# V on unnormalized probabilities, scaled later by reciprocals that pass through DRAM, in a top-k attention and SwiGLU kernel

## The chip, the core and the metric

The kernel runs on one core of a Trainium2 chip. TensorE (PE, with its weight loads as PEld), VectorE (DVE), ScalarE (ACT) and GpSimd (POOL) each work through their own instructions in order; SyncE (SP) issues nearly all DMAs. The metric is the device time of one execution in microseconds, given as the median of several runs.

## The reference

Inputs are q, k and v of 8 batches x 8 heads x 576 positions x 64, and three FFN weights. All is float32.

```python
scores = (q @ k.transpose(0, 1, 3, 2)) / np.sqrt(64)
kth = np.partition(scores, -32, axis=-1)[..., -32:-31]
scores = np.where(scores >= kth, scores, -1e9)          # the 32 largest of each row
scores = scores - scores.max(axis=-1, keepdims=True)
attn = np.exp(scores)
attn = attn / (attn.sum(axis=-1, keepdims=True) + 1e-9)
x = (attn @ v)            # (B,H,S,D) -> (B*S, H*D) = (4608, 512)
g = x @ w_gate            # 512 -> 1536
out = (g * sigmoid(g) * (x @ w_val)) @ w_out            # -> (4608, 512)
```

## The kernel before

**Units.** Attention is cut into 160 units: 8 batches x 5 query tiles x 4 pairs of heads. Query tiles 0 to 3 have 128 rows, and their units carry both heads of the pair, 1152 scores a row. Tile 4 has the last 64 rows; its two heads share the 128 partitions, so that unit is a "one-head" unit with 576 scores a row and half the work. In each batch 16 two-head units are followed by 4 one-head units.

**Steps of a unit.** `scores` (PE L308 or L294, copied to `sc` by ACT L313 or L299); `select` (DVE: four rounds of MAX8 L329 with three MATCH_REPLACE8 L333 between, for each head, then L339, which writes a large negative penalty into `e` where a score is below the 32nd); `penalize` (POOL L349, L351: adds the scores to the penalty); `weigh` (ACT exp L360 with the row sums in `tot`, and L365, which adds 1e-9); `normalize` (DVE reciprocal L372, ACT multiply L375, in place); `turn` (PE transposes L387 of the nine 128-column blocks of `e` into three PSUM tiles `etps`: four blocks, one, four; ACT copies L388 to `et`); `values` (PE L407 for the last 64 positions of both heads, L416 for the rest; ACT copy L431 into `xT`, the FFN's input).

**FFN.** `feed` works on blocks of 256 tokens. A block can begin when `values` has filled its `xT` for all four head pairs. Its matmuls are L471 (w_gate and w_val, 96 products of 128x128 by 256 columns, each two passes) and, behind block 0, seven quarters through L557 (42 products). ACT L496 to L503 and POOL L499, L504 and sums take the results. It is a generator: `pieces(n)` emits up to n pieces (four L471 products, or about that) while a credit lasts. `share(n)` gives the credit of a turn, about 6.4 pieces less the cost of PE's other work in it; a turn's unused credit is carried to a small extent, and nothing is emitted while no block is complete.

**Order.** The order on PE, DVE, ACT and POOL is that of the program: the last lines of the kernel chain each engine's instructions. SP's DMAs are placed by a scheduler. Turn n of the main loop (L729) emits `select` of unit n in parts, and beside it: at the head `penalize(n-1)`, `turn(n-3)`, `values(n-4)`, the scores of n+1, `weigh(n-1)`; then pieces, the reciprocal and multiplies of `normalize(n-2)`, key and query transposes for n+2 (`prep`, L255 to L268) where a new head pair begins, and more pieces. In the instruction order a two-head turn's tail and the next head read on PE: FFN, nine L387, L407 and eight L416 of the unit before, L308, FFN. The weights are rounded in the first turns (`rounded`, L105 to L123), by ACT, DVE and POOL.

**Buffers.** `sc` has 2, `e` 4, `et` 2, `tot` 3; PSUM has five tiles for attention (`ps_t`) and three for the FFN (`ps_f`).

Of the kernel before, what the change touches and what calls it, by code (L numbers as in the profile page):

```python
# [8 lines left out]
AF = mybir.ActivationFunctionType  # L9
# [6 lines left out]
P = 128  # L16
# [9 lines left out]
def kernel(  # L26
# [58 lines left out]
    ffn = ctx.enter_context(tc.tile_pool(name="ffn", bufs=2))  # L85
    ps_t = ctx.enter_context(tc.tile_pool(name="ps_t", bufs=5, space=PSUM))
    ps_f = ctx.enter_context(tc.tile_pool(name="ps_f", bufs=3, space=PSUM))

    ident = consts.tile([P, P], FP32, name="ident")
    make_identity(nc, ident[:])  # L90
# [2 lines left out]
    for i in range(NV):  # L93
        vt = consts.tile([P, P], FP32, name=f"vlast{i}")
        nc.vector.memset(vt[:], 0.0)
        vlast.append(vt)
    eps = consts.tile([P, 1], FP32, name="eps")
    nc.vector.memset(eps[:], EPS)
    wg = consts.tile([P, KC, DFF], FP32, name="wg")
    wv = consts.tile([P, KC, DFF], FP32, name="wv")  # L100
    wo = consts.tile([P, MC, DM], FP32, name="wo")
# [176 lines left out]
    def scores(n):  # L278
        b, qt, hp = units[n]
        slab = preps[b * NHP + hp]  # L280
        sc = work.tile([P, 2 * S], FP32, tag="sc", name="sc", bufs=2)
        halves = [slice(0, D), slice(D, P)]
        half = S // 2

        def bank():
            return ps_t.tile([P, 512], FP32, tag="t", name="s")


        if qt == J:
            banks = [bank() for _ in range(2)]  # L290
            for i, ps in enumerate(banks):
                for d in halves:
                    k0 = R + i * half
                    nc.tensor.matmul(  # L294
                        ps[d, 0:half], slab[d, S + R : S + 2 * R], slab[d, k0 : k0 + half]
                    )
            yield
            for i, ps in enumerate(banks):
                nc.scalar.copy(sc[:, i * half : (i + 1) * half], ps[:, 0:half])  # L299
        else:  # L300
            q0 = S + 2 * R + qt * P
            banks = []
            for i in range(2):
                for hh, d in enumerate(halves):
                    ps = bank()
                    banks.append((i + 2 * hh, ps))
                    k0 = (1 - hh) * R + i * half
                    nc.tensor.matmul(  # L308
                        ps[:, 0:half], slab[d, q0 : q0 + P], slab[d, k0 : k0 + half]
                    )  # L310
            yield
            for i, ps in banks:
                nc.scalar.copy(sc[:, i * half : (i + 1) * half], ps[:, 0:half])  # L313
        state[n] = dict(sc=sc)

    def select(n):

        nh = n_heads(units[n][1])
        sc = state[n]["sc"]
        m = small.tile([P, 2, TOP_K], FP32, tag="m", name="m", bufs=2)  # L320
        heads = [slice(t * S, (t + 1) * S) for t in range(nh)]
        rest = work.tile([P, 2 * S], FP32, tag="rest", name="rest", bufs=1)
        e = work.tile([P, 2 * S], FP32, tag="e", name="e", bufs=4)
        state[n] |= dict(m=m, e=e, heads=heads)
        cur = sc
        rounds = TOP_K // 8
        for r in range(rounds):
            for t, hs in enumerate(heads):
                nc.vector.max(m[:, t, 8 * r : 8 * r + 8], cur[:, hs])  # L329
                yield  # L330
            if r < rounds - 1:
                for t, hs in enumerate(heads):
                    nc.vector.match_replace(  # L333
                        rest[:, hs], m[:, t, 8 * r : 8 * r + 8], cur[:, hs], LOWEST
                    )
                    yield
                cur = rest
        for t, hs in enumerate(heads):
            nc.vector.tensor_scalar(  # L339
                e[:, hs], sc[:, hs], m[:, t, TOP_K - 1 : TOP_K], FAR, ALU.is_lt, ALU.mult  # L340
            )
# [12 lines left out]
    def weigh(n):  # L354

        st = state[n]
        e, heads, bias = st["e"], st["heads"], st.pop("bias")
        tot = small.tile([P, 2], FP32, tag="tot", name="tot")
        for t, hs in enumerate(heads):
            nc.scalar.activation(  # L360
                e[:, hs], e[:, hs], AF.Exp, bias=bias[:, t : t + 1], scale=scale,
                accum_out=tot[:, t : t + 1],
            )
        nh = len(heads)
        nc.scalar.activation(tot[:, 0:nh], tot[:, 0:nh], AF.Identity, bias=eps[:])  # L365
        st["tot"] = tot

    def normalize(n):
        st = state[n]
        tot, e, heads = st.pop("tot"), st["e"], st.pop("heads")  # L370
        nh = len(heads)
        nc.vector.reciprocal(tot[:, 0:nh], tot[:, 0:nh])  # L372
        yield
        for t, hs in enumerate(heads):
            nc.scalar.mul(e[:, hs], e[:, hs], tot[:, t : t + 1])  # L375

    def turn(n):

# [19 lines left out]
    def values(n):  # L398

        b, qt, hp = units[n]  # L400
        vt, v_last, vl = vs[b * NHP + hp]
        et = state.pop(n)["et"]
        last = qt == J
        ql = R if last else P
        av = ps_t.tile([P, P], FP32, tag="t", name="av")
        if not last:
            nc.tensor.matmul(av[:], vl[:], et[:, J, :], start=True, stop=False)  # L407
        for c in range(J + 1 if last else J):
            kl = R if c == J else P
            for hh in range(2):  # L410
                moving = (
                    et[0:kl, c, hh * R : (hh + 1) * R]
                    if last
                    else et[:, c + hh * (J + 1), :]
                )
                nc.tensor.matmul(  # L416
                    av[hh * R : (hh + 1) * R, 0:ql],
                    v_last[:, hh, :] if c == J else vt[:, hh, c, :],
                    moving,
                    start=last and c == 0,  # L420
                    stop=c == (J if last else J - 1),
                )
        c0 = b * S + qt * P
        at = c0
        while at < c0 + ql:
            kb = at // BLK
            n_c = min((kb + 1) * BLK, c0 + ql) - at
            if kb not in xT:
                xT[kb] = ffn.tile([P, NHP, BLK], FP32, tag="xT", name="xT", bufs=3)
                done[kb] = 0  # L430
            nc.scalar.copy(  # L431
                xT[kb][:, hp, at - kb * BLK : at - kb * BLK + n_c],
                av[:, at - c0 : at - c0 + n_c],
            )
            done[kb] += n_c
            at += n_c
# [265 lines left out]
    def pieces(n):  # L702
        for _ in range(n):
            if credit[0] >= 1:
                credit[0] -= piece()

    def run(steps):
        for _ in steps:
            pass

    def finish_unit(n):
        values(n)
        b, qt, hp = units[n]
        if qt == J and b + 1 < B:
            load_v((b + 1) * NHP + hp)
# [7 lines left out]
    run(fetch(1))  # L723
    credit = [0.0]
    no = iter(())
    over = {}
    TURN, VALUES = 3, 4
    due = [2.0]
    for n in range(NU + VALUES):  # L729
        nh = n_heads(units[n][1]) if n < NU else 1  # L730
        topk = select(n) if n < NU else no
        over[n - 1] = normalize(n - 1) if 0 <= n - 1 < NU else no
        nxt = scores(n + 1) if n + 1 < NU else no
        ahead = fetch(n + 2) if n + 2 < NU else no
        norm = over.pop(n - 2, no)

        def dve(k, beside=True):

            for _ in range(k * nh):
                next(topk, None)  # L740
                due[0] += 5 / 6 if beside else 0
                if due[0] >= 1:
                    due[0] -= 1
                    rounding(1)

        if n >= NU - NHP:
            credit[0] = 8.0
        else:
            credit[0] = min(credit[0] + share(n), share(n) + 1)
        flush(on_act)  # L750
        if 0 <= n - 1 < NU:
            penalize(n - 1)
        flush(on_pool)
        if 0 <= n - TURN < NU:
            run(turn(n - TURN))
        if n >= VALUES:
            finish_unit(n - VALUES)
        next(nxt, None)

        early[0]()  # L760
        if 0 <= n - 1 < NU:
            weigh(n - 1)
        run(nxt)


        dve(2, beside=False)
        if 2 <= n + 2 < NHP:
            load(n + 2)
        if n < NHP:
            load_v(n)  # L770
        pieces(2)
        flush(on_act)
        dve(1)
        dve(1)
        next(norm, None)
        run(norm)

        flush(on_pool)
        next(ahead, None)
        pieces(1)  # L780
        next(ahead, None)
        dve(1)
        pieces(1)
        dve(2, beside=False)
        run(topk)
        pieces(6)
    while piece():
        pass
# [48 lines left out]
```

## Time and profile before

| | |
|---|---|
| median of 3 runs | 1820.12 us (1819.79 to 1821.86) |
| profiled execution, first to last instruction | 1817.8 us |
| PE busy | 1708.7 us (94%) |
| DVE busy | 1610.7 us (89%) |
| ACT busy | 1218.7 us (67%) |
| POOL busy | 1036.4 us (57%) |
| mean granted TensorE clock | 0.967 |
| DMA | 59.65 MB, mean 33 GB/s |

The profiled execution shows its own span, 1817.8 us; what lies around it (start and end of the launch) is not in the page, and the median of the runs is 2.3 us above it. The page cuts the span into 40 slices of 45 us, each digit being the busy share in tenths. A timeline row reads: start in us, duration in us, engine, line, operation, output tile <- input tiles, sizes, xcount of merged instructions, and in brackets the engine's idle time just before with what ended it. Merged matmul rows overlap, since matmuls are pipelined: the pace is read from one row's start to the next row's start.

### The profile page before, as it was taken

Reading aid. Unit: us, or ns where it says so; the run is one execution under the profiler, and the core shown is the slowest. Engines: PE = TensorE matmul, PEld = TensorE weight load, DVE = VectorE, ACT = ScalarE, POOL = GpSimd, SP = SyncE. Lnnn points to the kernel's source line nnn. Section 1 sums busy time; section 2 is a strip of 40 time slices with the busy share of each in tenths; the row PEclk is TensorE's granted clock in tenths of the full one; section 3 lists DMA queues with packets and bytes.
Section 4 is the critical chain, followed back from the end, with each engine's and each line's share of the span. In section 5 each row is a group of like instructions: output and inputs, shape, how many; then the busy total and the mean of one; then the engine's idle time right before and its main releaser. Section 6 shows DMA issues by size and latency. Waiting matters only on the chain.

```text
span 1817.8 us, 30526 instructions
## 1 busy us (share of the span) xinstructions
PE 1708.7 (94%) x10756; PEld 1409.2 (78%) x10756; DVE 1610.7 (89%) x3372; ACT 1218.7 (67%) x2977; POOL 1036.4 (57%) x930
## 2 busy tenths in 40 slices
PE   4458999899999899999999999999999999999999
PEld 2346778687788788887888878887888878888887
DVE  7999999999999799997999989998999989998400
ACT  6778666676667676666767676767676766675532
POOL 5788756455565645554455636564556554646354
PEclk6669999899999999999999999999999999999999
DMA  7432030002100030000300021000300011000000
GB/s 191 125 108 90 14 85 7 12 1 50 45 1 13 2 82 12 13 1 22 73 12 2 13 56 39 1 12 3 74 19 13 1 36 33 1 13 12 1 12 12
DMA packets 109305, 59.65 MB, mean 33 GB/s; under 512 B 88544, under 2 KB 96992, under 8 KB 109152
## 3 DMA queue, kind: packets, MB, share of 16 engines
q1 hardware_dynamic: 108016, 57.37, 12.1%
q8 instruction: 85, 1.39, 0.3%
q14 instruction: 68, 0.56, 0.1%
q10 hardware_dynamic: 1136, 0.33, 0.1%
HBM read 48.23 MB, written 9.44 MB: 32 GB/s over the span
## 4 chain that ended last, share of the span: by engine, by line
PE 86%; DVE 8%; ACT 2%; POOL 2%; issue 2%; DMA 0%; SPq 0%; ACTq 0%; POOLq 0%
PE f L471 41%; PE x_ps L557 9%; PE av L416 8%; PE etps L387 7%; PE s L308 7%; PE y_ps L557 7%; DVE m L329 3%; DVE rest L333 3%; PE s L294 2%; PE av L407 1%; PE o_ps L517 1%; PE kqps L263 1%; DVE size L121 1%; DVE e L339 0%; POOL p L543 0%
## 5 line engine op out<-in xcount | busy, mean ns | idle before, releaser
L329 DVE MAX8 m<-rest 128x8 f32<-128x576 f32 x864 | 612.7, 744 | 2.2
L351 POOL TENSOR_TENSOR e<-e,sc 128x1152 f32<-128x1152 f32 (+1 forms) x160 | 383.1, 2394 | 83.7 <-DVE e L339 76.3
L333 DVE MATCH_REPLACE8 rest<-m,rest 128x576 f32<-128x576 f32 x576 | 423.1, 740 | 0.0
L471 PE MATMUL f<-xT,wg 128*128 128x256 f32 x1728 | 401.6, 382 | 0.0
L471 PE MATMUL f<-xT,wv 128*128 128x256 f32 x1728 | 399.1, 382 | 0.0
L471 PEld LDWEIGHTS f<-xT,wg 128*128 128x128 f32 x1728 | 323.1, 190 | 62.6 <-issue 21.3
L471 PEld LDWEIGHTS f<-xT,wv 128*128 128x128 f32 x1728 | 324.5, 190 | 58.7 <-issue 16.6
L499 POOL TENSOR_TENSOR h<-h,half_g 128x512 f32<-128x512 f32 x108 | 138.2, 1280 | 292.7 <-ACT h L498 292.2
L329 DVE MAX8 m<-sc 128x8 f32<-128x576 f32 x288 | 205.0, 747 | 104.0 <-ACT sc L299 57.8
L388 ACT COPY et<-etps 128x512 f32<-128x512 f32 (+1 forms) x448 | 184.1, 483 | 131.0 <-PE etps L387 130.2
L360 ACT ACTIVATE e<-e,bias 128x576 f32<-128x576 f32 x288 | 222.1, 777 | 57.5 <-POOL e L351 57.2
L387 PE MATMUL etps<-ident,e 128*128 128x128 f32 (+1 forms) x1312 | 184.5, 286 | 79.3 <-POOL size L122 18.2
L504 POOL TENSOR_TENSOR h<-h,val 128x512 f32<-128x512 f32 x108 | 139.6, 1293 | 186.3 <-ACT val L503 186.1
L387 PEld LDWEIGHTS etps<-ident,e 128*128 128x128 f32 (+1 forms) x1312 | 159.6, 147 | 106.0 <-POOL size L122 20.7
L375 ACT ACTIVATE e<-e,tot 128x576 f32<-128x576 f32 x288 | 212.0, 790 | 0.9 <-DVE tot L372 0.9
L333 DVE MATCH_REPLACE8 rest<-m,sc 128x576 f32<-128x576 f32 x288 | 211.5, 740 | 0.0
L308 PE MATMUL s<-kqT 64*128 64x288 f32 x1024 | 178.8, 449 | 14.1 <-ACT kqT L268 8.3
L339 DVE TENSOR_SCALAR e<-sc,m 128x576 f32<-128x576 f32 x288 | 177.2, 651 | 3.4
L416 PE MATMUL av<-et,v 128*64 128x128 f32 (+1 forms) x2560 | 170.3, 278 | 0.0
L313 ACT COPY sc<-s 128x288 f32<-128x288 f32 x512 | 164.0, 402 | 2.9 <-PE s L308 2.9
L496 ACT ACTIVATE h<-f 128x512 f32<-128x512 f32 x108 | 65.2, 604 | 133.3 <-PE f L471 133.3
L416 PEld LDWEIGHTS av<-et,v 128*64 128x64 f32 x2560 | 134.1, 143 | 22.8 <-issue 6.8
(73 smaller groups left out, 2029.1 us busy)
## 6 DMA issues: line engine op xcount, KB each, us to landing
v<-in_v_dram SPq DMA_DIRECT2D x32, 256.0 KB, 2.9
kq_in<-in_k_dram SPq DMA_DIRECT2D x63, 128.0 KB, 2.8
kq_in<-in_q_dram SPq DMA_DIRECT2D x63, 128.0 KB, 3.0
w<-in_moe_w_gate_dram SPq DMA_DIRECT2D x12, 512.0 KB, 3.7
w<-in_moe_w_val_dram SPq DMA_DIRECT2D x12, 512.0 KB, 3.8
w<-in_moe_w_out_dram SPq DMA_DIRECT2D x12, 512.0 KB, 3.5
out_dram<-o SPq DMA_DIRECT2D x38, 128.0 KB, 2.4
out_dram<-o SPq DMA_DIRECT2D x16, 256.0 KB, 2.4
```

Of the source, the lines that this page charges most:

```text
L308: nc.tensor.matmul(ps[:, 0:half], slab[d, q0 : q0 + P], slab[d, k0 : k0 + half])
L329: nc.vector.max(m[:, t, 8 * r : 8 * r + 8], cur[:, hs])
L333: nc.vector.match_replace(rest[:, hs], m[:, t, 8 * r : 8 * r + 8], cur[:, hs], LOWEST)
L339: nc.vector.tensor_scalar(e[:, hs], sc[:, hs], m[:, t, TOP_K - 1 : TOP_K], FAR, ALU.is_lt, ALU.mult)
L351: nc.gpsimd.tensor_tensor(e[:, every], e[:, every], sc[:, every], ALU.add)
L360: nc.scalar.activation(e[:, hs], e[:, hs], AF.Exp, bias=bias[:, t : t + 1], scale=scale, accum_out=tot[:, t : t + 1],)
L375: nc.scalar.mul(e[:, hs], e[:, hs], tot[:, t : t + 1])
L387: nc.tensor.transpose(ps[0:kl, c * P : (c + 1) * P], e[:, k0 : k0 + kl], ident[:])
L388: nc.scalar.copy(et[0:kl, c0 : c0 + cn, :], ps[0:kl, 0 : cn * P].rearrange("p (c j) -> p c j", c=cn),)
L416: nc.tensor.matmul(av[hh * R : (hh + 1) * R, 0:ql], v_last[:, hh, :] if c == J else vt[:, hh, c, :], moving, start=last and c == 0, stop=c ...
L471: nc.tensor.matmul(ps[:, i, :], w[:, kc, m * P : (m + 1) * P], x[:, kc, :], start=(kc == 0), stop=(kc == KC - 1),)
L557: nc.tensor.matmul(ps, lhsT, T[i][m], start=m == 0, stop=m == MQ - 1)
```

## The change

V is applied to the exponentials as they are, and its result is divided by the row sums later. `normalize` is gone, with L365 and the ACT multiplies L375. In its place:

- `invert(n)` adds 1e-9 and takes the reciprocal, both on DVE, and SP writes the 128x2 result to a DRAM tile of two rows of 128;
- `spread(n)` reads each row back from DRAM, broadcast over the 64 partitions of its head, into `inv` (128x128): two DMAs;
- `values` ends in an ACT copy to `avs` in place of the copy to `xT`;
- `scale_up(n)` multiplies `avs` by `inv` into `xT`, on POOL.

The main loop moves the steps: the transposes of unit n-1 now stand late in turn n, behind its `select` and ahead of the last `pieces`; `values(n-2)` and `spread(n-2)` stand at the head; `scale_up(n-3)` is POOL's first step of a turn, ahead of `penalize(n-1)`; `invert(n-1)` stands on DVE behind ten of a two-head unit's sixteen large operations (five of eight in a one-head unit). The loop has three turns behind the last unit in place of four. `sc` gets 3 buffers, `e` 2. The core of the diff:

```diff
-    eps = consts.tile([P, 1], FP32, name="eps")
-    nc.vector.memset(eps[:], EPS)
...
-        sc = work.tile([P, 2 * S], FP32, tag="sc", name="sc", bufs=2)
+        sc = work.tile([P, 2 * S], FP32, tag="sc", name="sc", bufs=3)
...
-        e = work.tile([P, 2 * S], FP32, tag="e", name="e", bufs=4)
+        e = work.tile([P, 2 * S], FP32, tag="e", name="e", bufs=2)
...
-        nc.scalar.activation(tot[:, 0:nh], tot[:, 0:nh], AF.Identity, bias=eps[:])
+    def invert(n):
+        st = state[n]
+        tot, heads = st.pop("tot"), st.pop("heads")
+        nh = len(heads)
+        nc.vector.tensor_scalar_add(tot[:, 0:nh], tot[:, 0:nh], EPS)
         nc.vector.reciprocal(tot[:, 0:nh], tot[:, 0:nh])
-        yield
-        for t, hs in enumerate(heads):
-            nc.scalar.mul(e[:, hs], e[:, hs], tot[:, t : t + 1])
+        row = dram.tile([2, P], FP32, tag="row", name="row")
+        if nh == 1:
+            nc.sync.dma_start(row[:, 0:R], tot[:, 0:1])
+        else:
+            nc.sync.dma_start(row[:].rearrange("h q -> q h"), tot[:])
+        st["row"] = row
+
+    def spread(n):
+        row = state[n].pop("row")
+        inv = small.tile([P, P], FP32, tag="inv", name="inv", bufs=2)
+        ql = R if units[n][1] == J else P
+        for hh in range(2):
+            nc.sync.dma_start(
+                inv[hh * R : (hh + 1) * R, 0:ql],
+                row[hh : hh + 1, 0:ql].to_broadcast([R, ql]),
+            )
+        state[n]["inv"] = inv
...
+        avs = small.tile([P, P], FP32, tag="avs", name="avs", bufs=2)
+        nc.scalar.copy(avs[:, 0:ql], av[:, 0:ql])
+        state[n]["av"] = avs
+
+    def scale_up(n):
...
-            nc.scalar.copy(
+            here = slice(at - c0, at - c0 + n_c)
+            nc.gpsimd.tensor_tensor(
                 xT[kb][:, hp, at - kb * BLK : at - kb * BLK + n_c],
-                av[:, at - c0 : at - c0 + n_c],
+                av[:, here], inv[:, here], ALU.mult,
             )
...
-    TURN, VALUES = 3, 4
+    TURN, VALUES, SCALE = 1, 2, 3
...
         flush(on_act)
-        if 0 <= n - 1 < NU:
-            penalize(n - 1)
+        if n >= SCALE:
+            scale_up(n - SCALE)
+        if behind:
+            penalize(n - TURN)
         flush(on_pool)
-        if 0 <= n - TURN < NU:
-            run(turn(n - TURN))
-        if n >= VALUES:
+        if VALUES <= n < NU + VALUES:
             finish_unit(n - VALUES)
+            spread(n - VALUES)
         next(nxt, None)
...
-        next(norm, None)
-        run(norm)
...
         dve(1)
+        if behind:
+            invert(n - TURN)
         pieces(1)
         dve(2, beside=False)
         run(topk)
+        if behind:
+            run(turn(n - TURN))
         pieces(6)
```

More of the change, by code (lines that the diff above doesn't have):

```diff
@@ L87 @@
     ps_f = ctx.enter_context(tc.tile_pool(name="ps_f", bufs=3, space=PSUM))
+    dram = ctx.enter_context(tc.tile_pool(name="dram", bufs=4, space=bass.MemoryType.DRAM))
     ident = consts.tile([P, P], FP32, name="ident")
@@ L363, in weigh @@
             )
+        st["tot"] = tot
+    def invert(n):
+        st = state[n]
+        tot, heads = st.pop("tot"), st.pop("heads")
         nh = len(heads)
-        nc.scalar.activation(tot[:, 0:nh], tot[:, 0:nh], AF.Identity, bias=eps[:])
[L366 to L371, printed above, removed]
-        nc.vector.reciprocal(tot[:, 0:nh], tot[:, 0:nh])
-        yield
-        for t, hs in enumerate(heads):
-            nc.scalar.mul(e[:, hs], e[:, hs], tot[:, t : t + 1])
+        nc.vector.tensor_scalar_add(tot[:, 0:nh], tot[:, 0:nh], EPS)
+        nc.vector.reciprocal(tot[:, 0:nh], tot[:, 0:nh])
+        row = dram.tile([2, P], FP32, tag="row", name="row")
[14 more added lines that the diff above has]
+        state[n]["inv"] = inv
     def turn(n):
@@ L401, in values @@
         vt, v_last, vl = vs[b * NHP + hp]
-        et = state.pop(n)["et"]
+        et = state[n].pop("et")
         last = qt == J
@@ L422, in values @@
                 )
+        avs = small.tile([P, P], FP32, tag="avs", name="avs", bufs=2)
+        nc.scalar.copy(avs[:, 0:ql], av[:, 0:ql])
+        state[n]["av"] = avs
+    def scale_up(n):
+        b, qt, hp = units[n]
+        st = state.pop(n)
+        av, inv = st["av"], st["inv"]
+        ql = R if qt == J else P
         c0 = b * S + qt * P
@@ L725 @@
     no = iter(())
-    over = {}
-    TURN, VALUES = 3, 4
+    TURN, VALUES, SCALE = 1, 2, 3
     due = [2.0]
-    for n in range(NU + VALUES):
+    for n in range(NU + SCALE):
         nh = n_heads(units[n][1]) if n < NU else 1
         topk = select(n) if n < NU else no
-        over[n - 1] = normalize(n - 1) if 0 <= n - 1 < NU else no
         nxt = scores(n + 1) if n + 1 < NU else no
         ahead = fetch(n + 2) if n + 2 < NU else no
-        norm = over.pop(n - 2, no)
+        behind = 0 <= n - TURN < NU
         def dve(k, beside=True):
@@ L750 @@
         flush(on_act)
-        if 0 <= n - 1 < NU:
-            penalize(n - 1)
+        if n >= SCALE:
+            scale_up(n - SCALE)
+        if behind:
+            penalize(n - TURN)
         flush(on_pool)
-        if 0 <= n - TURN < NU:
-            run(turn(n - TURN))
-        if n >= VALUES:
+        if VALUES <= n < NU + VALUES:
             finish_unit(n - VALUES)
+            spread(n - VALUES)
         next(nxt, None)
         early[0]()
-        if 0 <= n - 1 < NU:
-            weigh(n - 1)
+        if behind:
+            weigh(n - TURN)
         run(nxt)
@@ L785 @@
         run(topk)
+        if behind:
+            run(turn(n - TURN))
         pieces(6)
```

## The prediction

> **What bounds the kernel now.** I read the page first: busy shares, the 40 slices, the chain that ended last.
>
> ```profile
> PE   4458999899999899999999999999999999999999
> DVE  7999999999999799997999989998999989998400
> PE 86%; DVE 8%; ACT 2%; POOL 2%; issue 2%; DMA 0%; SPq 0%; ACTq 0%; POOLq 0%
> ```
>
> From slice 4 on both are nearly full, but the chain runs over PE for 86% of the span. So I looked for time in which PE waits at all, in PE's waits from 361 us to the end; the columns are total us, times, longest.
>
> ```profile
> PE etps L387 <- ACT e L375: 7.6, 6, 4.6
> PE etps L387 <- issue: 6.2, 6, 2.4
> ```
>
> These two, 13.8 us, are most of it (17 us) in 1457 us. Behind that point a us taken from PE is a us gained, and a us in which PE waits is a us lost; DVE, ACT and POOL have slack. Before 361 us it is otherwise. PE's timeline has, with no FFN work ready:
>
> ```profile
> 347.41 2.15 PE L387 MATMUL etps<-ident,e 128*128 128x128 f32 x9 [3.58 <-issue]
> 356.07 2.15 PE L387 MATMUL etps<-ident,e 128*128 128x128 f32 x9 [2.69 <-issue]
> 361.11 3.72 PE L471 MATMUL f<-xT,wg 128*128 128x256 f32 x16
> ```
>
> PE idles for DVE's units here and begins FFN block 2 at 361.11, so everything before is DVE's time (its shortest turn is 10.56 us: the first L329 of units 29, 30 and 31 at 338.57, 349.13 and 359.69). The span is this start plus PE's remaining work plus its waits.
>
> **One turn of PE, and what the new order does to it.** The timeline of PE and ACT:
>
> ```profile
> 912.78 1.15 PE L387 MATMUL etps<-ident,e 128*128 128x128 f32 x9
> 913.41 1.24 ACT L388 COPY et<-etps 128x512 f32<-128x512 f32 x3 [4.92 <-PE etps L387]
> 913.76 0.39 PE L407 MATMUL av<-et,vlast 128*128 128x128 f32 x2
> 914.07 1.09 PE L416 MATMUL av<-et,v 128*64 128x128 f32 x16
> 915.10 1.24 PE L308 MATMUL s<-kqT 64*128 64x288 f32 x8
> ```
>
> Today the V products at 913.76 belong to the unit whose transposes ran a turn earlier, so they follow the transposes without a pause while ACT copies. In the new order they belong to the very transposes just ahead. The first V product needs the middle copy, and the second head's products, from the third one of the turn on (due at about 914.21), need the last copy, which ends at 914.65. With 0.06 us for the semaphore PE goes on at 914.71: a wait of 0.5 us. Only work between the two covers it, and the instruction order of the new program shows where there is some: behind FFN block 2, of 103 two-head turns 61 have FFN matmuls there (at least 1.3 us, at 0.43 us for a product), 42 have none. 42 x 0.5 = **+21 us**. Queued behind the waiting product are the next scores, and behind them DVE's next unit, which has the slack.
>
> One-head turns: 24 there, 22 uncovered. Ten have transposes directly ahead of V: 0.6 us by the same rows (the first copy is longer than the transposes left), **+6 us**. In 12 the kqT transposes stand ahead, and their copies hold ACT:
>
> ```profile
> 649.18 0.71 PE L387 MATMUL etps<-ident,e 128*128 128x128 f32 x5
> 649.57 0.62 ACT L268 COPY kqT<-kqps 128x512 f32<-128x512 f32 x1
> 649.72 0.39 PE L407 MATMUL av<-et,vlast 128*128 128x128 f32 x2
> 650.05 0.76 ACT L388 COPY et<-etps 128x512 f32<-128x512 f32 x2
> ```
>
> V could go on at about 650.6 (first copy done) rather than 649.72: 12 x 0.9 = **+11 us**. Together +38; bounds 17 (0.4 a turn, one-head turns hidden) to 55 (0.23 more each if the pipe refills).
>
> Does the clock suffer from some 64 more short waits?
>
> ```profile
> 1050.00:1075.00 25.00, 23.48 (x178) 17.56 (x175) 19.43 (x38) 20.20 (x52) 9.27 (x11) 1.00 0.13 30
> 341.00:361.00 20.00, 13.73 (x100) 10.97 (x98) 20.00 (x43) 13.45 (x37) 6.53 (x5) 0.74 0.07 27
> ```
>
> Seventh column: the granted clock. The first window holds three PE waits of 0.37 to 0.67 us at clock 1.00; the second, with waits of 2.69 and 3.58 us, is at 0.74. I add nothing. The Trainium skill (TensorE: Matmul & The Clock Gate, section "A second HAM failure mode: psum-queue depth-cycling") says otherwise: frequent micro-idles between groups of matmuls can make the clock swing between half and full. By that rule, with one half-speed window of its 3.4 us behind each wait, the sum would be some 64 x 1.7 = 109 us higher, an estimate from that page; the first window speaks against it.
>
> **The start.** V is done two turns behind its unit instead of four, and scaled three behind, so block 2 is complete a turn earlier: at the head of turn 30, not 31. PE must first pass, behind the exp of unit 28 (345.1 us today), transposes, copies, V and scores at the slow rate of that stretch: 2.0 + 0.6 + 2.6 + 1.9 = 7.1 us, so FFN could resume at 352.2 instead of 361.1, with the same PE work left: **-9 us** (5 to 10). Against it: DVE gets a 128x2 add ahead of each reciprocal. L372 shows 152 ns, yet the next operation starts 0.08 us behind it; an add that the reciprocal must read costs 0.08 to 0.30, I take 0.15 (one L372), over 29 turns **+4 us** (2 to 9). Later turns have slack for it.
>
> **The waits that go.** The transposes wait today for the normalizing activations (L375, 288 x 0.79 us on ACT), which vanish. ACT's busy time is not on the path, but 13.8 us of PE's waits are: **-14 us** (6 to 17). In their place the transposes need the exp of the previous unit, in the same turn. Measured from a unit's scores to that exp's end against the PE work now ahead of the transposes, the margin is over 1 us except in three turns (56, 103, 129: -0.2 to -0.5 us), and the multiply that POOL gets ahead of its penalty add takes about 0.4 (between L349's 0.25 and the 0.75 of a 128x256 L543): **+3 us** (0 to 12).
>
> **Free moves.** The new wait on DVE (the reciprocal of unit n-1 behind ten of turn n's sixteen operations, about 7 us in) will often bite: where PE lags, exp n-1 ends 8 to 11 us into DVE's turn today, and the rest of the top-k queues behind it. But from that exp to the next it is 0.3 + 3.5 (rest of the turn) + 0.4 + 2.9 (POOL) + 2.0 (exps) = 9.1 us, under PE's 10.5 to 12.2 a turn, so it uses up DVE's idle time. The V copy goes on as an ACT copy (0.27). DRAM trip: three more DMAs a turn on SP; no row has such small runs. The nearest are vlast (16 KB, 2.0 us) and the largest load, 3.8; two in series are 4 to 8 us against a full turn from spread to use. If the cover goes, POOL's penalty, the exps and the transposes stand behind it. Once it has no cover: the last unit. Nothing is left for PE between its V and the last block, so exp, reciprocal, two DMAs and the multiply replace today's normalizing and copies: **+3 us** (0 to 8). SP's order puts key, value and store transfers between row and broadcast; full turns have room, one-head turns little.
>
> **Sum.** 38 - 9 + 4 - 14 + 3 + 3 = +25 us. The profiled span is 1817.8, and the median of the runs, 1820.1, lies 2.3 above it: 1817.8 + 25 + 2.3 = 1845. Its own bounds: 17 - 10 + 2 - 17 + 0 + 0 = -8 to 55 - 5 + 9 - 6 + 12 + 8 = +73.
>
> **Rivals.**
> - *Head start outweighs the new wait.* Faster: the earlier start and the vanished waits give 9 - 4 + 14 = 19 us, less 6 for the exps and the end, 13. It decides if a wait costs less than 13/64 = 0.2 us, as it would if the second head's products hid behind ACT's third copy. At 0.15 us: 64 x 0.15 - 13 = -3, 1817 us. For it: the ends of matmuls are modelled. Against: copies and products are starts that I subtract.
> - *DVE becomes the bound.* If L339 lands on POOL work as at 906.64 (2.48 us for two, 0.92 elsewhere), 9.1 becomes 10.7 us, and POOL's penalty waits for FFN products besides (up to 7.6 us behind its unit). With 0.5 us more for each of the 103 turns: 1845 + 52 = 1897. For: today's one spare turn between exp and reciprocal goes. Against: PE's turns are longer nearly everywhere.
> - *The DRAM trip shows in one-head turns.* Seven batches of four short turns, 1.2 us each lost in POOL: +34, 1879. For: SP's queue has a load waiting for PE ahead of the broadcast. Against: 5 to 6 us of turn against 4.
>
> **Chances.** The forecast 0.72, head start 0.10, DVE 0.10, DRAM trip 0.08. 0.2% is 3.6 us, about what a measurement of this kernel can tell from no change. Faster 0.06 and same 0.04 are the first rival's, with the forecast's low end adding 0.02 to same; slower 0.88. Range: 1820 to 1884, which leaves out most of the first rival and the worst of the DVE one.
>
> **What would show it.** PE's waits list L430 (the V products) behind ACT's et copies as the largest entry, 30 to 45 us, and the waits for normalizing are gone. The first FFN matmul after the starved turns starts near 355 us. DVE's waits show the new add behind ACT's exps, with no matching wait of PE. PE's clock stays near 1.00. Wrong would be: PE waiting over 20 us for exps or POOL (DVE or DRAM rival), V products with no wait, or the clock falling.

## The result, and the profile after

The changed kernel takes 2109.14 us (median of 4 runs, 2102.73 to 2116.22) against 1820.12 us: a ratio of 1.1585, 95% interval 1.1557 to 1.1613. The forecast was 1845 us, 1820 to 1884. It had the sign and missed the size by more than 260 us.

The same rows of the page (busy shares in 40 slices, now of 52.6 us each, then the chain that ended last):

```profile
PE   4448977798789987999789987999789996999979
DVE  8689866998679977899679976899679986999500
PE 41%; DMA 26%; POOL 9%; ACT 8%; DVE 8%; SPq 4%; issue 4%; POOLq 0%; ACTq 0%; DVEq 0%
PE f L496 23%; DMA row<-tot 12%; DMA inv<-row 9%; POOL e L350 4%; PE av L430 4%; PE s L307 4%; PE x_ps L582 4%; DVE m L328 3%; DVE rest L332 3%; PE etps L401 3%; PE y_ps L582 3%; ACT e L359 2%; SPq L385 2%; ACT et L402 2%; DMA w<-in_moe_w_val_dram 2%
```

The 8s and 9s of PE are broken by a 7 every few slices, one hole in each batch, and DVE has the same holes. DMA, which held 0% of the chain before, now holds 26%, and 21 points of that are the two halves of the trip: the write of the row and its read.

The waits name the queue. First SyncE's, then those of GpSimd and VectorE, which come later in the same chain of steps (total us, times, longest):

```profile
SPq L385 <- DMA row<-tot: 1222.4, 151, 11.4
POOL xT L456 <- DMA inv<-row: 441.4, 97, 15.5
DVE tot L370 <- ACT e L359: 299.0, 77, 13.0
```

And PE's, from 361 us on:

```profile
PE kqps L254 <- ACT sc L312: 57.7, 14, 11.6
PE etps L401 <- ACT e L359: 40.7, 12, 9.0
PE av L430 <- ACT et L402: 24.1, 23, 2.8
PE av L421 <- ACT et L402: 18.7, 43, 2.0
```

SyncE stands 8.1 us on average between a row's write and the read behind it: more than half of the span. The timeline of SyncE beside the three GpSimd steps that stand at the head of a turn:

```profile
907.04 0.38 SPq L376 DMA_DIRECT2D row<-tot  x1
916.06 1.08 SPq L385 DMA_DIRECT2D inv<-row  x2
...
919.86 0.46 POOL L456 TENSOR_TENSOR xT<-avs,inv 128x128 f32<-128x128 f32 x1
920.28 0.22 POOL L348 TENSOR_SCALAR bias<-m 128x2 f32<-128x2 f32 x1
921.50 2.64 POOL L350 TENSOR_TENSOR e<-e,sc 128x1152 f32<-128x1152 f32 x1 [1.01 <-DVE e L338]
```

Write issued at 907.04, read issued at 916.06, data used at 919.86 (the `...` stands for rows left out). A unit keeps SyncE for about 9 + 1 us in this manner, against two-head turns of 10.6 us and one-head turns of 6.2 us at their shortest before.

Where the 287.6 us of the two profiled spans lie, by the first MAX8 of each unit:

| | before | after | difference |
|---|---|---|---|
| start, to unit 31 | 359.7 | 440.9 | +81.2 |
| 101 two-head turns, units 31 to 155 | 1123.9 | 1257.3 | +133.4 |
| 24 one-head turns among them | 189.2 | 260.0 | +70.8 |
| from unit 156 to the end | 145.0 | 147.2 | +2.2 |

### The profile page after: what moved, and what is told of

Its sections match the earlier page's. It is cut to its first block, busy times and chain, and to the rows that moved or that the text cites. A ratio compares the mean times of both kernels' runs of the same rounds, so it can differ in the third digit from the quotient of the medians.

```text
span 2105.4 us, 31704 instructions
## 1 busy us (share of the span) xinstructions
PE 1795.0 (85%) x10756; PEld 1446.8 (69%) x10756; DVE 1665.2 (79%) x3531; ACT 974.9 (46%) x2497; POOL 1107.5 (53%) x1122
## 4 chain that ended last, share of the span: by engine, by line
PE 41%; DMA 26%; POOL 9%; ACT 8%; DVE 8%; SPq 4%; issue 4%; POOLq 0%; ACTq 0%; DVEq 0%
PE f L496 23%; DMA row<-tot 12%; DMA inv<-row 9%; POOL e L350 4%; PE av L430 4%; PE s L307 4%; PE x_ps L582 4%; DVE m L328 3%; DVE rest L332 3%; PE etps L401 3%; PE y_ps L582 3%; ACT e L359 2%; SPq L385 2%; ACT et L402 2%; DMA w<-in_moe_w_val_dram 2%
## 5 line engine op out<-in xcount | busy, mean ns | idle before, releaser
L496 PE MATMUL f<-xT,wg 128*128 128x256 f32 x1728 | 422.5, 395 | 11.0 <-POOL xT L456 11.0
L496 PE MATMUL f<-xT,wv 128*128 128x256 f32 x1728 | 406.4, 385 | 0.0
L496 PEld LDWEIGHTS f<-xT,wg 128*128 128x128 f32 x1728 | 334.4, 198 | 81.3 <-issue 24.5
L456 POOL TENSOR_TENSOR xT<-avs,inv 128x128 f32<-128x128 f32 (+1 forms) x192 | 78.9, 418 | 444.5 <-DMA inv<-row 441.4
L370 DVE TENSOR_SCALAR tot<-tot 128x2 f32<-128x2 f32 (+1 forms) x160 | 44.8, 280 | 314.0 <-ACT e L359 299.0
L401 PE MATMUL etps<-ident,e 128*128 128x128 f32 (+1 forms) x1312 | 194.4, 292 | 81.9 <-ACT e L359 63.9
L430 PE MATMUL av<-et,v 128*64 128x128 f32 (+1 forms) x2560 | 181.4, 287 | 28.2 <-ACT et L402 28.2
L338 DVE TENSOR_SCALAR e<-sc,m 128x576 f32<-128x576 f32 x288 | 184.8, 678 | 5.3 <-DVE m L328 1.4
L430 PEld LDWEIGHTS av<-et,v 128*64 128x64 f32 x2560 | 143.7, 150 | 55.5 <-ACT et L402 36.6
```

The source lines that it names most:

```text
L338: nc.vector.tensor_scalar(e[:, hs], sc[:, hs], m[:, t, TOP_K - 1 : TOP_K], FAR, ALU.is_lt, ALU.mult)
L401: nc.tensor.transpose(ps[0:kl, c * P : (c + 1) * P], e[:, k0 : k0 + kl], ident[:])
L430: nc.tensor.matmul(av[hh * R : (hh + 1) * R, 0:ql], v_last[:, hh, :] if c == J else vt[:, hh, c, :], moving, start=last and c == 0, stop=c ...
L496: nc.tensor.matmul(ps[:, i, :], w[:, kc, m * P : (m + 1) * P], x[:, kc, :], start=(kc == 0), stop=(kc == KC - 1),)
```

## The experiments

All are the changed kernel with the edit shown (the core of it; `...` stands for lines left out), beside runs of the kernel before on the same chip. `wide_row` and `scale_late` ran once, so they have no interval; the four versions of the write ran twice, the others four times or more.

### Without the trip, and with a wider write

`no_trip`:

```diff
-        row = dram.tile([2, P], FP32, tag="row", name="row")
...
-                row[hh : hh + 1, 0:ql].to_broadcast([R, ql]),
...
-        state[n]["inv"] = inv
+        state[n]["inv"] = ones
```

> The changed kernel without its DRAM trip: the add and the reciprocal stay on DVE, but the row write and the two broadcast reads are left out, and POOL multiplies by a constant tile (so the rows are not divided by their own sums). Theory A (the trip through DRAM is what makes the changed kernel slow, and the rest is as in the forecast): 1835 to 1865 us, PE's V products waiting 30 to 45 us behind the et copies. Rival B (the new order itself, DVE's reciprocal waiting for the exp of the same turn, is the bound): over 1950 us.

`wide_row`:

```diff
-        nc.vector.reciprocal(tot[:, 0:nh], tot[:, 0:nh])
+        wide = wides[n % 4]                    # 128x128 constants
+        nc.vector.reciprocal(wide[:, 0:nh], tot[:, 0:nh])
...
-            nc.sync.dma_start(row[:].rearrange("h q -> q h"), tot[:])
+        nc.sync.dma_start(row[:], wide[0:2, :])
```

> The same DMAs at the same places, but the row write moves two runs of 512 bytes from a constant-filled tile that the reciprocal writes two columns of, in place of 256 (one-head: 128) runs of 4 bytes (so the rows are not divided by their own sums). Theory A1 (the write lands late because of its 4-byte runs): SP's wait for it falls from 8.1 us to 2 to 3 us each, and the time to 1850 to 1920 us. Rival A2 (any write to DRAM that is read back lands that late): the wait stays near 8 us and the time near 2100 us.

Measured: 1870.45 us without the trip (ratio 1.027, interval 1.025 to 1.029) and 1873.36 us with the wide write. The first lies 5 us above theory A's range and far below rival B's; the second is in A1's. So the trip costs 2109 - 1870 = 239 us, and the rest of the change 48 us (49.5 by the spans, 1867.3 against 1817.8). The second kernel has every DMA in its place and only the shape of the write changed; SyncE's wait for it (the read is L388 there):

```profile
SPq L388 <- DMA row<-wide: 119.5, 143, 3.0
SPq L379 <- DVE wide L377: 937.9, 136, 14.3
```

That is 0.84 us in place of 8.1, less than the 2 to 3 expected. What costs is not a trip through DRAM, but this write. The second row shows that standing alone is no price either: SyncE waits 938 us for reciprocals ahead of its writes, and the kernel is only 3 us slower than without a trip. The change differs in that a unit then needs SyncE for about 10 us, which is nearly a two-head turn and more than a one-head turn, so the queue falls behind and the loads with it.

### More turns for the trip

`scale_late` scales a turn later; `spread_late` is that, and its program emits the read a turn later as well:

```diff
-        inv = small.tile([P, P], FP32, tag="inv", name="inv", bufs=2)
+        inv = small.tile([P, P], FP32, tag="inv", name="inv", bufs=3)
-        avs = small.tile([P, P], FP32, tag="avs", name="avs", bufs=2)
+        avs = small.tile([P, P], FP32, tag="avs", name="avs", bufs=3)
-    TURN, VALUES, SCALE = 1, 2, 3
+    TURN, VALUES, SCALE = 1, 2, 4
...
-            spread(n - VALUES)
+        if VALUES < n <= NU + VALUES:          # spread_late alone
+            spread(n - VALUES - 1)
```

> The scaling four turns behind top-k in place of three, with a third buffer for inv and avs; the broadcast reads are issued where they were, so SP still stands behind the row write in each turn. Theory A3 (the trip's latency in the loop exp, reciprocal, row, broadcast, multiply, penalty, exp sets the turns): a turn of slack takes it off, 1850 to 1920 us. Rival A4 (SP's queue, blocked for 8 us and more behind each row write, sets the turns): little changes, 2030 to 2110 us.

> As scale_late, and the broadcast reads also issued a turn later, when the row has landed. Theory A3 and rival A4 both expect the slowdown of the trip to go, 1840 to 1890 us: neither SP nor POOL stands behind a row write any more. Rival B expects over 1950 us.

Measured: 1997.99 and 2012.5 us. The first lies between its theories, 78 us above A3's range and 32 below A4's. The second is 122 us above the range that A3 and A4 shared; it is in rival B's (over 1950), but `no_trip`, with the same order of steps and 1870 us, had already excluded that. The one-head turns came back (24 of them take 181.6 and 183.8 us, against 260.0), but the second turn of batches 1 to 7 takes 19 to 31 us (10.6 to 12.6 before), and the start stays long (unit 31 at 417.9 and 420.9). In `spread_late`:

```profile
SPq L385 <- DMA row<-tot: 1161.3, 152, 9.7
PE kqps L262 <- DMA kq_in<-in_k_dram: 59.0, 8, 12.5
```

SyncE still stands between write and read. SyncE's order in the trace says why: it is the scheduler's, and it has nearly every read still directly behind the write of the same row, though the program emits it a turn later. So `spread_late` did not do what it was made for. The second row shows a cost that the consumer's slack can't hide: key and query loads queue behind the standing read.

### The trip on ScalarE's queue

`act_queue` moves the three DMAs to ScalarE's queue in program order, with the extra buffers and SCALE 4; `slack` also has the old order of transposes and V (V of one unit right behind the transposes of the next), with the buffers that it needs:

```diff
-            nc.sync.dma_start(row[:].rearrange("h q -> q h"), tot[:])
+            nc.scalar.dma_start(row[:].rearrange("h q -> q h"), tot[:])   # put(n - 2)
...
-            nc.sync.dma_start(
+            nc.scalar.dma_start(                                         # spread(n - 3)
                 inv[hh * R : (hh + 1) * R, 0:ql],
```

> The changed kernel with its trip through DRAM on ScalarE's DMA queue in program order, and with slack: the row of unit n-2 is written at the head of turn n, read back at the head of the next turn, and used a turn after that (SCALE 4, three inv and avs buffers, four tot). SyncE carries only loads and stores again. Theory 1 (what the late scaling left over, some 130 us above the kernel without the trip, is SyncE's in-order queue standing about 8 us behind each row write, with key, value and weight loads behind it): 1865 to 1895 us, SyncE's waits for row are gone, and no wait of PE for kq_in. Theory 2 (the extra transfers themselves cost it, wherever they are issued): 1950 us or more.

> All parts of the result are computed. The old order of transposes and V products (transposes of unit n-2 at the head of turn n, V of n-3 right behind them, so V never follows its own transposes), with the new scaling in place of normalizing: add and reciprocal of n-2 early on DVE, the row written from ScalarE's queue, read back a turn later, scaled at n-4. Theory 1 (the trip is harmless with a turn of slack on a queue that nothing else needs, and V waits only for its own transposes): 1800 to 1818 us, since the 13.8 us of waits for normalizing are gone. Theory 2 (three DMA issues a turn on ScalarE hold up its copies): 1825 to 1870 us.

Measured: 2041.35 us (ratio 1.1211, interval 1.1194 to 1.1227) and 2356.07 us (ratio 1.2935, interval 1.2904 to 1.2965). The first is in theory 2's range (1950 or more), though not for its reason as far as is shown here; the second is 486 us above the higher theory's range. ScalarE's rows in `act_queue`:

```profile
905.29 1.10 ACTq L391 DMA_DIRECT2D inv<-row  x2
906.48 0.54 ACTq L382 DMA_DIRECT2D row<-tot  x1
907.07 0.78 ACT L359 ACTIVATE e<-e,bias 128x576 f32<-128x576 f32 x1 [1.58 <-DMA inv<-row]
```

The issues alone hold ScalarE 1.6 us a unit, ahead of the exps that VectorE and PE wait for, and wherever a landing is late, the exps now wait for it. This kernel doesn't tell SyncE's share from the transfers' own, so the next two were made. In `slack` the trip closes a loop through two in-order engines:

```profile
ACT e L359 <- POOL e L350: 885.2, 148, 11.3
POOL xT L462 <- DMA inv<-row: 843.3, 144, 13.4
```

GpSimd waits for the read; ScalarE's exp waits for GpSimd's next step; the next write and read stand behind that exp on ScalarE.

### A trip for which only SyncE waits

`idle_trip` keeps all DMAs of the change; GpSimd reads a constant:

```diff
-                av[:, here], inv[:, here], ALU.mult,
+                av[:, here], ones[:, here], ALU.mult,
```

`idle_write` leaves the read out as well.

> The changed kernel with its DMAs as they are (row written, read back into inv on SyncE), but GpSimd multiplies by a constant tile, so no engine waits for the trip: only SyncE does. Theory 1 (what late scaling left over is SyncE's in-order queue, held about 8 us by each row write, with loads behind it): 1985 to 2015 us, with PE waiting for key and query loads in the second turn of each batch and a start some 40 us longer than without the trip. Theory 2 (the consumer's wait was all of it, and late scaling failed for another reason): 1868 to 1890 us.

> The changed kernel with the row written to DRAM (256 runs of 4 bytes) but never read back; GpSimd multiplies by a constant tile. Theory 1 (SyncE stands because the read must wait for the write to land): with no read behind it SyncE goes on, 1870 to 1895 us. Theory 2 (the small runs themselves slow the other transfers): over 1950 us, as with the read.

Measured: 2102.55 us (ratio 1.154, interval 1.1522 to 1.1557), as large a loss as that of the change, with no consumer at all. So it doesn't need GpSimd's 441 us of waits. What waits in its place:

```profile
SPq L387 <- DMA row<-tot: 1306.7, 151, 11.2
PE kqps L264 <- DMA kq_in<-in_k_dram: 126.8, 13, 21.6
ACT e L361 <- DMA row<-tot: 96.8, 23, 8.9
```

Loads come late (second turns of 26 to 31 us), and the exps wait for the row write of three units before, since it has to have read the `tot` buffer that they write. Theory 1 has the mechanism; its range, 1985 to 2015 us, is missed by 88 us.

Two things stay open here. The loss lies elsewhere than in the change: the second turns lose more, and the 24 one-head turns take 230.5 us against 260.0. And `idle_trip` is 105 us slower than the one run of `scale_late`, where GpSimd does wait for the trip: SyncE stands 1307 us for rows against 1164 there, as the two-head write takes 9.3 us until the read against 8.3. Why the same write takes longer in one program than in the other is not shown.

`idle_write` takes 1930.92 us, between the two theories: with nothing to read, SyncE still has 51 us of waits for rows, most of them here:

```profile
SPq L243 <- DMA row<-tot: 37.4, 12, 7.6
```

L243 loads V. In the trace SyncE's DMAs share eight completion semaphores in turn, and one which takes a semaphore up again waits for its last user. So of the 60 us above `no_trip` some is still SyncE standing; how the rest divides isn't shown.

### The order without the trip

`no_trip_v3` is `no_trip` with V a turn later; `no_trip_no_add` is `no_trip` without the two small steps on VectorE:

```diff
-    TURN, VALUES, SCALE = 1, 2, 3
+    TURN, VALUES, SCALE = 1, 3, 4              # no_trip_v3
...
-        nc.vector.tensor_scalar_add(tot[:, 0:nh], tot[:, 0:nh], EPS)     # no_trip_no_add
-        nc.vector.reciprocal(tot[:, 0:nh], tot[:, 0:nh])
```

> The kernel without the row and inv DMAs (constant multiplier in their place), and with the V products three turns behind top-k in place of two, so that PE has the scores and FFN products of a turn between a unit's transposes and its V products (SCALE 4). Theory 1 (the remaining 48 us over the kernel before are mainly V products that wait for the copies of their own transposes): 1820 to 1840 us, PE's waits of L408 and L417 for et nearly gone, the first FFN block 2 a turn later (about +8 us at the start). Theory 2 (the add and reciprocal on DVE, which wait for the exps): over 1855 us.

> The kernel without the row and inv DMAs, and without the add and reciprocal on DVE as well (constant multiplier; the row sums are made and not used). V products two turns behind, as in the change. Theory 1 (V products waiting for copies): only the starved start gets shorter, by 5 to 15 us: 1855 to 1866. Theory 2 (DVE's wait for the exps with the rest of the top-k behind it): 1820 to 1840 us.

Measured: 1817.86 us (ratio 0.9985, interval 0.9976 to 0.9995) and 1863.86 us (ratio 1.0235, interval 1.0219 to 1.025). Theory 1 holds in both; the first is 2 us below its range, and its FFN block 2 begins 3.9 us later than in `no_trip` (368.9 against 364.9), where 8 were expected. PE's waits from 361 us on, in `no_trip`:

```profile
PE av L417 <- ACT et L389: 20.6, 23, 1.9
PE av L408 <- ACT et L389: 16.6, 42, 2.0
PE etps L388 <- ACT e L360: 10.5, 6, 3.9
```

and in `no_trip_v3`:

```profile
PE etps L388 <- ACT e L360: 11.5, 6, 4.7
PE av L417 <- ACT kqT L268: 2.8, 5, 0.7
```

One turn between the transposes and their V takes the waits away, and the 48 us with them.

### What makes the write slow

Four versions of `idle_trip`, which differ in what is written to the row (the read behind it stays two DMAs of 64x128):

```diff
+        nc.sync.dma_start(row[0:1, 0:32].rearrange("o q -> q o"), tot[0:32, 0:1])                # few_runs
+        nc.sync.dma_start(row[:].rearrange("h (q t) -> (h q) t", t=2), wide[:, 0:2])             # pairs
+        nc.sync.dma_start(row[:].rearrange("h (q t) -> (h q) t", t=16), wide[:, 0:16])           # lines
+            nc.sync.dma_start(row[:, 0:1].rearrange("(q h) o -> q (h o)", h=2), tot[:])          # spaced
```

> The version in which only SyncE waits for the trip (GpSimd multiplies by a constant tile), with only the first 32 reciprocals of a unit written, as 32 runs of 4 bytes next to each other in DRAM. From issue of the write to issue of the read behind it, which took 9.3 us with 256 such runs. Theory 1 (the number of runs sets the landing): about 1.5 to 3 us, and 1870 to 1920 us in all. Theory 2 (each small write into a line that others write too is slow): 3 to 9 us. Theory 3 (any 4-byte run costs a fixed 8 us): about 9 us, about 2100 us.

> As few_runs, but with both reciprocals of a partition beside each other: 128 runs of 8 bytes, together 1 KB without gaps. Theory 1 (number of runs): about 5 us from write to read. Theory 2 (shared lines): 8 to 9 us, since 64 runs fall into each 512 bytes as in the one-head write. Theory 3 (4-byte runs alone): below 3 us.

> As few_runs, but 128 runs of 64 bytes, together 8 KB without gaps (the first columns hold the reciprocals, the others a constant). Theory 1 (number of runs): about 5 us from write to read. Theory 2 (runs that share a 64-byte line): below 3 us. Theory 3 (4-byte runs alone): below 3 us.

> As few_runs, but all 256 runs of 4 bytes, each 512 bytes from the next in DRAM. Theory 1 (number of runs): about 9 us from write to read and some 2100 us in all. Theory 2 (neighbours in one line): below 4 us, and 1870 to 1950 us. Theory 3 (any 4-byte run): about 9 us.

From issue of the write to issue of the read directly behind it, mean over the units of a run:

| write | runs x bytes, place in DRAM | us | whole kernel, us |
|---|---|---|---|
| `idle_trip`, two-head | 256 x 4, adjacent | 9.3 | 2102.55 |
| `idle_trip`, one-head | 128 x 4, adjacent | 9.9 | |
| `few_runs` | 32 x 4, adjacent | 3.5 | 1879.96 |
| `pairs` | 128 x 8, adjacent | 3.3 | 1878.07 |
| `lines` | 128 x 64, adjacent | 1.6 | 1872.08 |
| `spaced` | 256 x 4 (128 in one-head units), 512 bytes apart | 2.1 | 1876.05 |
| `wide_row` | 2 x 512 | 1.2 | 1873.36 |

`spaced` decides it. It has as many runs of 4 bytes as the change, and SyncE's wait is all but gone:

```profile
SPq L393 <- DMA row<-tot: 200.6, 146, 2.9
```

Neither the number of runs nor their size makes 9 us by itself; that many small runs next to each other in DRAM do. Theory 3 falls, and theory 1 too (256 runs in 2.1 us, and 128 adjacent ones are no faster than 256). Theory 2 holds in kind, but not as a rule by lines: 128 adjacent runs of 4 bytes take 9.9 us and 128 of 8 bytes 3.3, which none of the three theories had, and no run here shows why.

### A version that beats both

`dve_row` computes the whole result. Beside the edit it has three buffers of `inv` and `avs`, and its 128x32 `tot` tiles are set to 1 once, so that the transpose reads nothing undefined:

```diff
-        nc.vector.tensor_scalar_add(tot[:, 0:nh], tot[:, 0:nh], EPS)
-        nc.vector.reciprocal(tot[:, 0:nh], tot[:, 0:nh])
+        nc.vector.transpose(flat[:], tot[:])               # 128x32, in 32x32 blocks
+        nc.vector.reciprocal(flat[:], flat[:])
+        row = dram.tile([8, 32], FP32, tag="row", name="row")
+        for t in range(nh):
+            nc.sync.dma_start(row[4 * t : 4 * t + 4], flat[t : P : 32])
...
-    TURN, VALUES, SCALE = 1, 2, 3
+    TURN, VALUES, SCALE = 1, 3, 4
...
+        if 0 <= n - 2 < NU:                                # behind dve(2)
+            invert(n - 2)
+            spread(n - 2)
```

`dve_row_mid` is that with VALUES 2 and SCALE 3, and both steps moved to the middle of the turn.

> A complete version. The sums are laid out as rows on chip first: VectorE transposes a 128x32 tile of which the sums fill the first two columns, in 32x32 blocks, and takes the reciprocal of the result; so a head's 128 reciprocals go to DRAM in four runs of 128 bytes in place of 128 of 4 (two writes and two reads a unit). V products three turns behind, scaling four, both DVE steps at the head of the turn after the one of the exps. The 1e-9 is left out (the largest term of each sum is 1, so float32 rounds it away). Theory 1 (the trip is dear through 4-byte runs only, V through its own transposes): 1812 to 1826 us. Theory 2 (any trip through DRAM holds SyncE's queue): 1860 us or more.

> As the version with the sums transposed on VectorE, but the V products of unit n-2 in the middle of turn n, behind the scores and up to two FFN pieces, and the scaling of n-3 in the middle of turn n. Theory 1 (V waits only where nothing lies between it and its transposes; a block is complete half a turn earlier, so the starved start ends earlier): 1803 to 1822 us. Theory 2 (a turn from the sums to their use is too little for the trip, above all in one-head turns): 1830 to 1880 us.

Measured: `dve_row` 1812.9 us, a ratio to the kernel before of 0.9951, interval 0.9936 to 0.9965: half a per cent, small but clear of 1. Two lines of its page, then SyncE's wait for the write (the read is L390 there):

```profile
PE   5567999799999999999999999999999999999999
PE 71%; DVE 20%; POOL 3%; issue 3%; ACT 2%; DMA 1%; SPq 0%; ACTq 0%; POOLq 0%; DVEq 0%
```

```profile
SPq L390 <- DMA row<-flat: 66.9, 129, 1.5
```

DMA holds 1% of the chain, though the trip has more DMAs than in the change (four a two-head unit). `dve_row_mid` takes 1846.5 us (ratio 1.0139, interval 1.0122 to 1.0155), a miss for theory 1 and in theory 2's range. But the trip isn't the cause: SyncE's wait for rows is 66.0 us, and GpSimd waits 13.5 us for the reads against 15.7 in `dve_row`. PE's waits from 361 us on are 20 us against 18, yet PE is busy 1458 us there against 1430, for about as many matmuls (9163 and 9155). The clock is little of that: in the trace it is at half for 18 us of this stretch against 10, worth some 4 us. The rest stays open.

## Why the prediction was wrong

**The step that failed: "DRAM trip".** It stood among the free moves: "two in series are 4 to 8 us against a full turn from spread to use". Two errors are in that sentence. The size came from rows with large runs (vlast, 16 KB, 2.0 us), when the text itself said that no row has such small runs; the write alone took 8.7 us in the changed kernel (two-head units, mean of 116, issue to read). And the room was taken as that of the consumer, "from spread to use", when the transfer is also a wait on SyncE, in order, ahead of every load; "full turns have room" was said of the transfers on it, not of its time. `idle_trip` shows that the wait on SyncE alone, with nobody using the data, makes as large a loss (2103 us), and `wide_row` that it does so only because the write is long (1873 us with a short one in its place). The term was 0, and it is 238 us (spans of `no_trip` and after).

**The third rival was the right mechanism in too small a place.** It had SyncE's queue and the one-head turns at 1.2 us each, +34. One-head turns lost 70.8 us, or 2.9 each; the start, which it left out, lost 81.2, and the second turns of batches 1 to 7, which it left out too, take 11.5 to 24 us where they took 10.6 to 12.6. Its "against: 5 to 6 us of turn against 4" rested on the same size of the write.

**The V products.** Forecast 64 waits and 38 us; `no_trip` shows 65 waits and 20.6 + 16.6 = 37.2 us. Counting the uncovered turns in the instruction order was right, by kind too: 42 waits are of two-head units (L408; 16.6 us against 21), 23 of one-head units (L417; 20.6 against 17). Their price is higher than their length: `no_trip_v3` is 51.0 us shorter in span. From 361 us on PE waits 21.4 us there against 51.3, which is 30 us, and is busy 1432.2 against 1451.0, which is 19 us, for as many matmuls (9155 and 9161). Of the 19 the clock explains some 7 (below). The other 12 would be 0.19 us a wait, near the 0.23 that the forecast kept for its upper bound ("if the pipe refills"), but no run separates them. In the changed kernel the same two waits are 42.8 us, as the forecast's test asked (30 to 45), but no longer the largest: PE waits 57.7 us for score copies ahead of key transposes and 40.7 for exps. The second is over the 20 that the text named as a sign that it was wrong.

**The clock.** The forecast took the row (clock near 1.00) against the rule. `no_trip`, with its 65 waits, has a mean clock of 0.961 in the profiled run, `no_trip_v3` 0.966, but their other runs overlap (0.960 to 0.965 and 0.961 to 0.966). From 361 us on the trace of `no_trip` has half the clock in six stretches, 25 us in all, that of `no_trip_v3` in three, 11 us in all: some 7 us more lost, where the forecast added nothing. The Trainium skill's rule (TensorE: Matmul & The Clock Gate, "A second HAM failure mode: psum-queue depth-cycling") would have given 109 by the forecast's own estimate. The swing between half and full that it names is there, but in six places and not behind each of the 65 waits. In the changed kernel the clock is 0.918, with PE waiting for long stretches: a consequence, which goes when the trip is mended (`dve_row` 0.964).

**The start.** Forecast -9 + 4. Without the trip, FFN block 2 begins at 364.9 us against 361.1: +4. A turn earlier in the program was right, but the turns got longer: 11.9 and 13.9 us where they were 11.5 and 13.4, in part by the two small steps on VectorE (11.6 and 13.6 without them), of which I had put the new one, the add, at 0.15; and units 10 to 14 took 13.6, 15.9, 12.8, 16.3 and 13.4 where they took 11.5, 14.3, 12.8, 14.4 and 12.7; why these are longer is not shown (without the two steps units 11 to 13 still take 15.7, 15.4 and 16.0). Without the two steps block 2 begins at 358.8 us, so the head start is 2 us in place of 9 and the steps cost 6 there in place of 4; over the whole span the kernel gains 4.9 us.

**The vanished waits.** Forecast -14, and +3 for exps in their place. The waits for normalizing are gone, but the transposes of `no_trip` wait 10.5 us for exps from 361 us on. Net -3 in place of -11.

**The end.** Forecast +3; +2.2 in the change, and -8 without the trip (137.3 against 145.0 us from unit 156 to the end).

**The other rivals.** The head start didn't outweigh the waits. VectorE waits 299 us for exps in the changed kernel, 118.6 us in `no_trip`, yet leaving its steps out of `no_trip` gave 4.9 us: it didn't become the bound there.

The sum without the trip would have been +25 against +49.5, inside its own bounds of -8 to +73; that is in part luck, since its terms missed in both directions (V and the start above the forecast, the end below). With the trip the range could not hold: the text allowed write and read together 8 us at most, and only GpSimd's chain and the one-head turns to pay.

## What to carry to other kernels

A DMA that waits for another DMA holds the whole in-order queue that issues it: price it by the time that a unit then needs the queue, transfer included, against the turn and against all that is issued behind it, and not only by the slack of whoever uses the data. A write to DRAM in many small adjacent runs must be measured before it is placed; laying the values out as rows on chip first (a small block transpose here) took SyncE's wait from 8.1 to 0.5 us a unit, and with V a turn later the whole kernel came out 0.5% faster than before, where the change had lost 16%. And a step that moves closer to its producer needs the work of at least one other step between them, counted in the instruction order of the built program.

## What the runs showed of the hardware

- The 4-byte packets of the write issued at 907.04 us had all ended by 908.2, but its 16 completion signals came between 913.1 and 916.0. The Trainium skill (DMA: Bandwidth & Descriptors, "Anatomy of one DMA — SWDGE (gpsimd) path") says of DMAs on GpSimd's path that their fixed cost of about 2 us is mostly the wait until the last byte is confirmed in the target memory; this DMA is issued by SyncE, and its trace agrees on the place, after the packets, but shows 5 to 8 us.
- The same 256 runs of 4 bytes, 512 bytes apart, let the read go 2.1 us after the write was issued, and 9.3 us when adjacent.
- In `act_queue`, at 905 us, issuing DMAs holds ScalarE 0.54 us for the write and 1.10 us for the two reads.
